# Filler products on TensorE: placed in waits up to 110 in the plan's time, or only up to 30

## The chip, the cores and the metric

One core of a Trainium2 chip runs the kernel. The metric is the device time of one execution in microseconds (us), read as the median of several runs of the same kernel.

## The reference

Attention over a pooled, projected key/value grid, and then a mixture of eight experts in which each token goes to one of them. Four batches of 12,288 tokens of 128 numbers; 768 keys per batch.

```python
kv_pool = kv.reshape(B, H // r, r, W // r, r, C).mean(axis=(2, 4))
k = v = kv_pool.reshape(B, -1, C) @ w_sr
s = scale * (q @ k.transpose(0, 2, 1))
a = np.exp(s - s.max(-1, keepdims=True)); a /= a.sum(-1, keepdims=True) + 1e-09
x = (a @ v).reshape(B * S, D)
logits = x @ w_gate; e = np.argmax(logits, axis=1); gate = softmax(logits)[e]
y = gate[:, None] * (np.maximum(x @ w1[e], 0.0) @ w2[e])
```

## The kernel before

The tokens are cut into 96 blocks of 512 (`block`, 24 per batch). For each block the scores against the 768 keys are made on TensorE in three steps of two products of 512 columns each (`scores`, written to a pair of PSUM banks `s`, of which there are two). ScalarE makes the exponential `e` of a pair (L1020), VectorE combines pair and exponential to `r` (L1022), and the values are then summed on TensorE into `po` (`values`). VectorE or ScalarE copy `po` out as `xp` (L1056, L1057), a transposing DMA turns it, and the expert's two layers follow on TensorE (`hidden`, `rows`, banks `b`, of which there are two as well). All matrix products but the transposes go through one helper, so they share line L387 and are told apart by their tiles.

Ahead of the blocks stands the preparation of batch 0: its keys are loaded, summed and turned (`keys`), giving `vT`, then `KT` (L548, VectorE), which the first scores need. The expert of the batch is guessed and its weights are loaded and rearranged (`expert`) while the first blocks already run: `b<-wg_raw,cbc` (the guess), `s<-ident,raw` (L694, the weights turned), `b<-kr` (a square of the keys), `b<-u,ones`, `b<-cg,vT`, `s<-Ms,raw`, and at about 80 us `PU` (L795, a 0/1 matrix that picks columns of the weights) with the products that gather through it.

The order of the work on every engine is fixed when the kernel is built. Each step is an `Op` with an engine, a planned duration and a due time; `Plan.order` runs a small simulation of the five engines and takes, engine by engine, the step that can start first. The times of this plan are its own, not the chip's.

Filler products belong to this plan. `fill` (L1526) makes three products of `slots16` with itself, 384 columns each, into a bank `b` that nobody reads. When `Plan.order` has picked the next step of TensorE with a start time `start` before `filler_end`, it first puts in as many groups of three as fit between the time at which TensorE becomes free and `start` (L208 to L221), at .487 us of plan time each. On the chip the fillers stand in TensorE's queue like any product: a real product behind them starts when they are through and when its own waits have ended. Each group takes one of the two banks `b` in the plan, so the choice of bank for later steps can swap.

```python
            if o.eng == "PE" and self.filler and start < self.filler_end:
                make, fill, us = self.filler
                while free["PE"] > self.filler_start:
                    i = min(range(len(slots["b"])), key=lambda i: slots["b"][i])
                    at = max(free["PE"], slots["b"][i])
                    if at + us > start:
                        break
```

Of the kernel before, what the change touches and what calls it, by code (L numbers as in the profile page):

```python
# [268 lines left out]
def attention_moe(ctx: ExitStack, tc, q, kv, w_sr, w_gate, w1, w2, out):  # L269
# [132 lines left out]
    plan = Plan({**SBUF, **PSUM})  # L402
# [3 lines left out]
    def buf(pool, shape, dtype=F32):  # L406
        where = psum if pool in PSUM else sb
        return Buf(pool, lambda name: where.tile(shape, dtype, name=name))

    def bank():  # L410
        return buf("b", [P, 512])
# [1115 lines left out]
        for _ in range(3):  # L1527
            mm(b.tile[:, :UN], slots16[:, :P], slots16, True, True)

    plan.filler, plan.filler_start, plan.filler_end = (bank().make, fill, .487), 9.0, 110.0  # L1530
    with tc.manual_schedule():
        plan.issue()

# [28 lines left out]
```

## Time and profile before

| what | value |
|---|---|
| time, median of 3 runs | 786.45 us (785.96 to 789.99) |
| the profiled execution's own time | 786.58 us |
| its span, first to last instruction | 784.5 us |
| granted TensorE clock, mean of the span | 0.998 |
| TensorE (PE) busy | 739.5 us, 94% |
| VectorE (DVE) busy | 639.1 us, 81% |
| ScalarE (ACT), GpSimd (POOL) busy | 588.0 us, 577.3 us |

The span is the profiled execution without launch and end, 2.1 us less than its time. Products are pipelined: a product's row gives the time from its start to its modelled end, so products that follow each other closely overlap in these rows, and the pace is read from their starts. The granted clock is a share of 2.4 GHz; 0.5 of it is the lower level, 1.2 GHz.

### The profile page before, as it was taken

The numbers are of one execution on the slowest core, as the hardware profiler recorded it, in microseconds if no ns is written. First come the engines' busy times: TensorE is split into PE (matmuls) and PEld (weight loads), VectorE is DVE, ScalarE is ACT, GpSimd is POOL, SyncE is SP. The second block draws the span as 40 slices with busy tenths as digits, with TensorE's granted clock in tenths as the row PEclk, the third lists the DMA queues.
The fourth block names the chain that finished last, engine by engine and source line by source line (L and its number), as shares of the span: only waits on it lengthen the run. The fifth ranks groups of instructions, "written<-read, shape, count | busy, mean of one in ns | idle before, by whom it ended". The sixth has DMA issues, their size and how long they took to land.

```text
span 784.5 us, 21744 instructions
## 1 busy us (share of the span) xinstructions
PE 739.5 (94%) x8399; PEld 580.3 (74%) x8399; DVE 639.1 (81%) x1262; ACT 588.0 (75%) x968; POOL 577.3 (74%) x803
## 2 busy tenths in 40 slices
PE   5997999999999899999999899999999999999995
PEld 5675776887777677778776776878877777787774
DVE  5789876889988888868968888688898898767685
ACT  1367778879778777777787787778878787878783
POOL 0357879878789888886779978888656957686662
PEclk9999999999999999999999999999999999999999
DMA  9676989995798999797569899799575889668441
GB/s 341 166 204 115 223 191 204 198 199 114 156 231 175 228 205 264 154 210 134 122 139 225 205 240 248 158 192 192 136 166 106 171 176 200 151 122 166 93 105 56
DMA packets 326168, 138.90 MB, mean 177 GB/s; under 512 B 212478, under 2 KB 318082, under 8 KB 326064
## 3 DMA queue, kind: packets, MB, share of 16 engines
q1 hardware_dynamic: 325584, 137.27, 78.0%
q8 instruction: 66, 1.08, 0.6%
q14 instruction: 38, 0.31, 0.1%
q0 software_dynamic: 192, 0.17, 0.1%
q10 hardware_dynamic: 288, 0.07, 0.0%
HBM read 59.12 MB, written 26.94 MB: 110 GB/s over the span
## 4 chain that ended last, share of the span: by engine, by line
PE 64%; DVE 9%; ACT 8%; DMA 8%; POOL 5%; issue 3%; SPq 0%; ACTq 0%; POOLq 0%; DVEq 0%
PE b L387 31%; PE po L387 19%; PE s L387 13%; DMA qT<-qp 4%; DVE r L1022 4%; ACT e L1020 3%; POOL kv L478 1%; DMA x<-xp 1%; DMA kv<-in_kv_dram 1%; DMA gp<-in_q_dram,gi 1%; ACT X L1113 1%; ACT g L1121 1%; DVE y L1148 1%; DVE xp L1057 1%; ACT junk L742 1%
## 5 line engine op out<-in xcount | busy, mean ns | idle before, releaser
L1022 DVE SCALAR_TENSOR_TENSOR r<-s,e 128x1024 bf16<-128x1024 f32 x288 | 346.8, 1217 | 63.7 <-ACT e L1020 61.6
L1020 ACT ACTIVATE e<-s 128x1024 f32<-128x1024 f32 x288 | 292.1, 1029 | 62.6 <-PE s L387 59.0
L387 PE MATMUL po<-v,r 128*128 128x145 f16 x2304 | 251.4, 227 | 2.6 <-DVE xp L1057 1.7
L387 PEld LDWEIGHTS <-r 128*128 128x128 bf16 x2304 | 167.0, 98 | 26.7 <-issue 4.9
L387 PE MATMUL s<-qT,KT 128*128 128x512 f16 x576 | 166.8, 379 | 11.6 <-DVE r L1022 7.7
L387 PE MATMUL b<-w2U,g 128*128 128x128 f16 x1664 | 156.5, 219 | 1.0 <-POOL g L1117 0.6
L387 PE MATMUL b<-x,w1U 128*128 128x512 f16 x465 | 139.4, 379 | 9.0 <-ACT g L1121 4.7
L387 PE MATMUL po<-M,qT 128*128 128x136 f16 x1152 | 130.9, 223 | 0.0
L387 PE MATMUL b<-L,x 128*128 128x128 f16 x1116 | 123.0, 219 | 1.1 <-ACT g L1121 0.7
L1003 POOL TENSOR_TENSOR qp<-qr,qp 128x512 f16<-128x512 f32 x94 | 108.9, 1159 | 15.6 <-DVE gi L1314 2.0
L1117 POOL TENSOR_TENSOR g<-X,g 128x512 f16<-128x512 f32 x94 | 108.8, 1158 | 10.8 <-DVE gg L1451 4.1
L387 PEld LDWEIGHTS <-g 128*128 128x128 f16 x1664 | 109.0, 98 | 1.9 <-POOL g L1117 1.4
L387 PEld LDWEIGHTS <-qT 128*128 128x128 f16 x1152 | 84.5, 98 | 27.6 <-issue 5.1
L1121 ACT ACTIVATE g<-b,zb 128x512 f16<-128x512 f32 x128 | 87.5, 692 | 18.3 <-PE b L387 15.3
L1001 POOL CAST qp<-qr 128x512 f16<-128x512 f32 x94 | 58.7, 625 | 47.7 <-DMA qr<-in_q_dram 25.3
L387 PEld LDWEIGHTS <-x 128*128 128x128 f16 x1116 | 80.9, 98 | 16.8 <-issue 5.4
L387 PEld LDWEIGHTS <-KT 128*128 128x128 bf16 x576 | 51.3, 99 | 48.0 <-issue 14.1
L1113 ACT ACTIVATE X<-b,zb 128x512 f32<-128x512 f32 x94 | 65.2, 696 | 19.5 <-PE b L387 19.5
L478 POOL TENSOR_TENSOR kv<-kv,kv 128x512 f32<-128x512 f32 x54 | 68.0, 1272 | 15.4 <-DMA kv<-in_kv_dram 6.1
L1115 POOL CAST g<-X 128x512 f16<-128x512 f32 x94 | 58.2, 620 | 28.3 <-ACT X L1113 13.1
L387 PEld LDWEIGHTS <-w1U 128*128 128x128 f16 x480 | 45.2, 98 | 40.5 <-issue 9.2
L1148 DVE TENSOR_TENSOR y<-b,gt 128x512 f32<-128x512 f32 x96 | 65.2, 680 | 7.8 <-PE b L387 5.8
(376 smaller groups left out, 961.2 us busy)
## 6 DMA issues: line engine op xcount, KB each, us to landing
qr<-in_q_dram SPq DMA_DIRECT2D x96, 256.0 KB, 3.4
out_dram<-y SPq DMA_DIRECT2D x96, 256.0 KB, 2.7
kv<-in_kv_dram SPq DMA_DIRECT2D x41, 512.0 KB, 6.1
raw<-in_moe_w_dram SPq DMA_DIRECT2D x14, 512.0 KB, 5.1
e<-in_kv_dram SPq DMA_DIRECT2D x3, 512.0 KB, 9.1
v_dram<-vT SPq DMA_DIRECT2D x4, 384.0 KB, 3.1
qT<-qp SPq DMA_TRANSPOSE x94, 3.6
x<-xp SPq DMA_TRANSPOSE x91, 3.5
```

Source lines behind the costliest of these rows:

```text
L387: return nc.tensor.matmul(o, l, r, start=start, stop=stop)
L478: nc.gpsimd.tensor_add(flat(to), flat(to), flat(of))
L742: op("ACT", 1.25, lambda j=j, junk=junk: nc.scalar.activation(junk.tile, krow.tile, AF.Sign, bias=key(j), scale=-1.0, accum_out=lc(j)), at ...
L1001: op("POOL", .62, lambda: nc.gpsimd.tensor_copy(qp.tile[:, 0], qr.tile), T - 1.9 * LEN, [("qr", t)], [("qh", t)], [qr, qp])
L1003: op("POOL", 1.17, lambda: nc.gpsimd.tensor_sub(qp.tile[:, 1], qr.tile, qp.tile[:, 0]), T - 1.8 * LEN, [("qh", t)], [("qp", t)], [qr, qp])
L1020: op("ACT", 1.03, lambda e=e, ps=ps: nc.scalar.activation(e.tile, ps.tile, AF.Exp), at + .6, [("s", t, s)], [("e", t, s)], [ps, e])
L1022: op("DVE", 1.22, lambda e=e, ps=ps, s=s: nc.vector.scalar_tensor_tensor(r.tile[:, 2 * s:2 * s + 2], ps.tile, 1.0, e.tile, op0=ALU.add, op ...
L1113: op("ACT", .69, lambda ph=ph, zu=zu: nc.scalar.activation(gf.tile, ph.tile, AF.Relu, bias=zu()), at + .5, [("ph", t, u), ("zb", b)], [("g ...
L1115: op("POOL", .62, lambda: nc.gpsimd.tensor_copy(gg.tile[:, 0], gf.tile), at + 1.5, [("gf", t)], [("gh", t), ("g", t)], [gf, gg])
L1117: op("POOL", 1.16, lambda: nc.gpsimd.tensor_sub(gg.tile[:, UH], gf.tile, gg.tile[:, 0]), at + 2, [("gf", t), ("gh", t)], [("g", t)], [gf, gg])
L1121: op("ACT", .69, lambda u=u, ph=ph, zu=zu: nc.scalar.activation(gg.tile[:, u], ph.tile, AF.Relu, bias=zu()), at + .5, [("ph", t, u), ("zb" ...
L1148: op("DVE", .69, lambda: nc.vector.tensor_tensor(y.tile, py.tile.rearrange("p (c d) -> p c d", d=C), bc(gr["gt"].tile[:, 0, js], C), op=AL ...
```

## The change

One number: `filler_end` goes from 110.0 to 30.0, in the plan's time. Steps of TensorE that start at 30 or later in the plan get no fillers ahead of them.

```diff
-    plan.filler, plan.filler_start, plan.filler_end = (bank().make, fill, .487), 9.0, 110.0
+    plan.filler, plan.filler_start, plan.filler_end = (bank().make, fill, .487), 9.0, 30.0
```

TensorE's queue has 28 groups of fillers before and 6 after: 22 groups, 66 products with their 66 weight loads, are left out. The other instructions of TensorE and all those of the other engines stand in the same order. From the place below on, the banks `b0` and `b1` are exchanged in all later steps, each for the other, with the same pattern of use.

TensorE's queue at the first scores of batch 0 (`u`: the scale of the keys; `KT`, `qT`: keys and queries of block 0; `slots`: the filler's operand), before:

```order
L387 LDWEIGHTS ones_b
L387 MATMUL b_325<-u_310,ones_b 128x128
L387 LDWEIGHTS slots_84
L387 MATMUL b_343<-slots_84 128x384
...
L387 MATMUL b_355<-slots_84 128x384
L387 LDWEIGHTS KT_338
L387 MATMUL s_359<-qT_295,KT_338 128x512
```

and with the change:

```order
L387 LDWEIGHTS ones_b
L387 MATMUL b_325<-u_310,ones_b 128x128
L387 LDWEIGHTS KT_338
L387 MATMUL s_343<-qT_295,KT_338 128x512
L387 LDWEIGHTS KT_338
```

Four groups (b_343, b_347, b_351, b_355) are gone, and the first scores stand right behind the product that they were separated from.

TensorE's queue between the guess of the expert and the third pair of scores (`qT_316`: queries of block 1), before:

```order
L387 MATMUL s_364<-qT_316,KT_338 128x512
L387 MATMUL b_372<-wg_raw,cbc_362 128x8
L387 LDWEIGHTS slots_84
L387 MATMUL b_402<-slots_84 128x384
...
L387 MATMUL b_414<-slots_84 128x384
L387 LDWEIGHTS KT_338
L387 MATMUL s_418<-qT_316,KT_338 128x512
```

and with the change:

```order
L387 MATMUL s_348<-qT_316,KT_338 128x512
L387 MATMUL b_356<-wg_raw,cbc_346 128x8
L387 LDWEIGHTS KT_338
L387 MATMUL s_386<-qT_316,KT_338 128x512
L387 LDWEIGHTS KT_338
```

Again four groups are gone. The same holds ahead of the next scores (1, 4, 1 and 3 groups), behind the values of block 0 (3 groups) and on both sides of a pair of scores just ahead of the gather through `PU` (1 and 1).

## Rows read from the trace of the kernel before

**Rows 1.** The page: the span, TensorE's share of it, and its granted clock.

```profile
span 784.5 us, 21744 instructions
...
PE 739.5 (94%) x8399; PEld 580.3 (74%) x8399; DVE 639.1 (81%) x1262; ACT 588.0 (75%) x968; POOL 577.3 (74%) x803
...
PEclk9999999999999999999999999999999999999999
```

**Rows 2.** Timeline of PE, 28 to 45 us: start, duration, line, tiles, count, [idle before].

```profile
28.51 0.23 PE L387 MATMUL b<-u,ones_b 128*128 128x128 bf16 x1 [0.20 <-DVE u L520]
29.22 2.33 PE L387 MATMUL b<-slots 128*128 128x384 f16 x12 [0.48 <-DVE con L523]
31.39 1.03 PE L387 MATMUL s<-qT,KT 128*128 128x512 f16 x4
32.25 0.28 PE L387 MATMUL b<-wg_raw,cbc 128*128 128x8 f32 x2
32.39 2.54 PE L387 MATMUL b<-slots 128*128 128x384 f16 x12
34.83 0.59 PE L387 MATMUL s<-qT,KT 128*128 128x512 f16 x2
...
36.39 2.11 PE L387 MATMUL b<-slots 128*128 128x384 f16 x12
38.34 0.59 PE L387 MATMUL s<-qT,KT 128*128 128x512 f16 x2
...
41.52 1.09 PE L694 MATMUL s<-ident,raw 128*128 128x128 f32 x8
```

**Rows 3.** Stretches: length, busy (instructions) of PE, PEld, DVE, ACT, POOL, clock, DMA, GB/s.

```profile
28.50:41.50 13.00, 12.25 (x66) 6.36 (x66) 11.68 (x28) 7.13 (x8) 8.21 (x11) 1.00 0.87 219
41.50:48.70 7.20, 6.91 (x63) 5.92 (x62) 4.93 (x12) 5.34 (x11) 2.79 (x4) 1.00 1.00 332
```

**Rows 4.** The same view for PE's filler products alone.

```profile
28.50:41.50 13.00, 9.73 (x51) 1.00 0.87 219
```

**Rows 5.** The chain of waits, 28 to 45 us: start, duration, what.

```profile
36.55 1.95 PE b L387 x12
```

**Rows 6.** Timeline of DVE: steps that TensorE waits for at 31.4, 38.3, 81.6 us.

```profile
30.04 1.07 DVE L548 TENSOR_SCALAR KT<-vT,con 128x256 bf16<-128x256 f32 x1
...
37.05 2.35 DVE L1022 SCALAR_TENSOR_TENSOR r<-s,e 128x1024 bf16<-128x1024 f32 x2
...
80.58 1.08 DVE L795 TENSOR_SCALAR PU<-slots,sg 128x384 f16<-128x384 f16 x4
```

**Rows 7.** Timeline of ACT and of DVE at 39 to 45 us.

```profile
39.20 1.92 ACT L1020 ACTIVATE e<-s 128x1024 f32<-128x1024 f32 x2
...
44.45 0.16 DVE L818 TENSOR_SCALAR ws<-b 128x2 f32<-128x2 f32 x1 [1.86 <-PE b L387]
```

**Rows 8.** Timeline of PE at 81 us.

```profile
81.14 0.65 PE L387 MATMUL b<-slots 128*128 128x384 f16 x3
81.62 0.61 PE L387 MATMUL b<-PU,w1l 128*128 128x128 f16 x8
```

**Rows 9.** Groups of PE, 8.4 to 13.05 us and 15.4 to 17.2 us: count, busy, mean ns, idle.

```profile
L387 PE MATMUL s<-ident,kv 128*128 128x128 f32 x20 | 4.9, 431 | 5.3 <-DVE kv L463 5.3
...
L387 PE MATMUL s<-ident,kv 128*128 128x128 f32 x16 | 1.9, 275 | 0.0
```

**Rows 10.** Timeline of PE, its last products.

```profile
778.39 0.61 PE L387 MATMUL b<-lp,ones 128*128 128x9 f32 x4
```

**Rows 11.** Stretches at the end of the span, columns as in rows 3.

```profile
775.00:780.00 5.00, 3.57 (x54) 3.13 (x51) 3.81 (x11) 0.00 (x0) 0.68 (x3) 1.00 0.16 44
780.00:785.00 5.00, 0.00 (x0) 0.00 (x0) 0.48 (x3) 0.00 (x0) 0.00 (x0) 0.61 0.21 66
```

**Rows 12.** PE's waits over the whole span: us in total, times, longest.

```profile
PE s L387 <- DVE r L1022: 7.7, 8, 1.7
...
PE s L387 <- DVE kv L463: 5.3, 1, 5.3
```

## The prediction

> **What bounds the kernel now.** I read the page first. TensorE (PE) is busy for 94% of the span and its clock row shows nines from end to end [rows 1]: over most of its length the kernel is paced by TensorE, and whatever delays it early is likely to be still there at the end. The change touches the first 82 us alone, so I went to the timeline of PE there, to see what stands around the fillers [rows 2]. Between 28.5 and 41.5 us TensorE is busy for 12.25 of 13 us [rows 3], but 9.73 us of that are 51 filler products [rows 4], 17 of the 22 groups that go. Real work is 15 products: the one at 28.51, four scores at 31.39, two at 32.25 and four pairs of scores, 0.23 + 1.03 + 0.28 + 4 x 0.59 = 3.9 us by their durations [rows 2]. So this stretch is not bound by TensorE.
>
> The chain of waits seems to say otherwise: it names a filler stretch, twelve products at 36.55, as part of the path [rows 5]. The reader should not believe it before looking at the other side of the wait. The scores at 38.34 [rows 2] reuse a bank pair that VectorE frees with the first of two steps that start at 37.05 and take 2.35 us together [rows 6]; half of that is 38.2, about 0.1 us ahead of the scores. VectorE releases them; the filler only happened to end last. From 41.5 to 48.7 us it is different: 6.91 of 7.2 us are real products [rows 3], without one filler, and VectorE sits idle for 1.86 us before it gets what it needs from there [rows 7]. That stretch is bound by TensorE.
>
> **The change, part by part.**
>
> *The products themselves.* In plan time 22 x .487 = 10.7 us of work go. They lay in waits, so I cost nearly all of it at nothing. The cover is the wait itself, and I look for places where the filler outlasts it. At 31.39 the first scores start [rows 2], while their keys are ready at 30.04 + 1.07 = 31.11 [rows 6]: at most 0.28 us, less the 0.1 us that a start takes behind its release at 38.34. At 81.62 the gather through PU starts behind a group that began at 81.14 [rows 8]; the gather's eight products need all pieces of PU, and the last four of these are done at 80.58 + 1.08 = 81.66 [rows 6]. Its eighth product starts at about 81.62 + 7 x 0.06 = 82.0 (the row's 0.61 us less a last product of some 0.2, over seven steps); without fillers it could start at about 81.75, so 0.25 us is the most that comes free. I take 0.2 us of gain in all; the ends are 0 (VectorE is just as late) and 0.5 (both places in full). The exchange of the two banks b0 and b1 changes no wait, for each keeps its partner's pattern: 0. The weight loads that go run beside the products: 0.
>
> *The clock.* This is the term that can cost. What the lower level is worth shows at the start of the span. The first 20 products of 128 columns, behind a wait of 5.3 us, take 431 ns each and fill 4.9 us, 0.24 us apiece; 16 of the same kind at 15.4 us take 275 ns and fill 1.9 us, 0.12 apiece [rows 9]. That is the pace of 1.2 GHz against 2.4 GHz, although the clock row shows full there as well (nothing is recorded ahead of the first change). It took from 8.4 to about 13 us of products before the pace rose.
>
> When does it fall? The trace shows one fall. The last products end at 778.39 + 0.61 = 779.0 [rows 10]; the granted clock is 1.00 up to 780 and 0.61 on average over the five us that follow [rows 11], which is 1.0 for 1.1 us and 0.5 for the rest. So it fell to 1.2 GHz at 781.1, 2.1 us after the last product. At the other end, no wait at full clock was longer than 1.7 us [rows 12], and none of those made it fall. The fillers gone, TensorE waits from 28.74 to about 31.3 us (2.6 us), from 32.5 to 34.83 (2.3 us), from about 36.5 to 38.34 (1.8 us) [rows 2], and again for shorter times. Two waits longer than the 2.1 us that sufficed at the end, one after another, with hardly any work between: I expect a fall somewhere between 31 and 36 us.
>
> A rule that speaks against this change stands in the Trainium skill, page "TensorE: Matmul & The Clock Gate", section "A second HAM failure mode: psum-queue depth-cycling": where products come in groups with short pauses between, the clock swings between its two levels although no pause is long. By that rule the sum holds the clock term below, and without it the gain of 0.2 us alone.
>
> *What the lower level costs.* First, the pairs of scores. Four columns' worth of 512 take 32.25 - 31.39 = 0.86 us [rows 2], 0.215 us each, so a pair ends 0.43 us later at half pace (an estimate by doubling). Most of this is hidden: the next exponential or VectorE's step has other work in front of it. Where it isn't is the pair at 38.34, whose exponential starts at 39.20 [rows 7]; the pair would end at 39.36 instead of 38.93 and the exponential start some 0.2 us late, and with it VectorE's step and the transposes at 41.52, which wait for that step's bank: +0.2 us (ends 0 and 0.4).
>
> Second, the stretch from 41.52, where TensorE has products without a gap and everybody waits for it. As long as the lower level lasts there, half of the time is lost. How long it lasts is the unknown. It could rise at once (0 lost), or need as long as at the start, 4.6 us, until 46.3 us: 2.3 us lost. I take 43.5 us, near the middle: 1.0 us lost. What is late then is the pair of scores at 42.65, the transposed weights' copy and VectorE's step at 44.45, and by them the values of block 0 at 48.8. Behind it both VectorE and TensorE are nearly full, so I let the 1.0 us through to the end.
>
> *The sum*: -0.2 + 0.2 + 1.0 = +1.0 us on the profiled execution's 786.58 us, 787.6 us. That execution is 0.13 us above the median of 786.45, so for the median I say **787.5 us**, 0.13% more. About 0.5% (3.9 us) is what a measurement of this kernel can tell from no change, so this would read as no difference.
>
> **The rivals.**
>
> *The clock stays up.* For it: all the new waits but two are shorter than the 2.1 us of idleness that stood ahead of the fall, and those two exceed it by little. Against it: no wait at full clock was longer than 1.7 us, so nothing shows that 2.6 us is borne. Then only the first term counts: 786.58 - 0.2 = 786.4 us, between 786.1 and 786.6.
>
> The same page of the Trainium skill, in "Why this matters for your kernels", warns of single idle gaps, and of long ones only. By that rule the clock would stay and this rival hold; the trace agrees in so far as 1.7 us did no harm.
>
> *Slower by more than 0.5%: the clock falls twice and comes back late.* The waits between 28.7 and 41.5 cost the whole of the unknown, 0.4 + 2.3 = 2.7 us with no gain. Then it falls again: three filler groups behind the values of block 0 go too, and a little later the scores wait for VectorE anyway (the 7.7 us in eight waits [rows 12]). A second return as slow as the first, 4.6 us with TensorE some two thirds busy, costs half of 3 us, 1.5 us. Together +4.2 us, 790.8 us. It decides from the point where the level is still low beyond 46 us and low again at a second place. Against it: behind 41.5 TensorE is as busy as it was at 8.4 to 13 us, so it should have recovered, and in the trace it kept its clock through all these later waits.
>
> *The change does something else than it says.* The order on all five engines speaks against it: only fillers are gone. What is left is chance in the transfers when everything shifts by a fraction of a us, which I can't price; within 1 us either way.
>
> **How the numbers follow.** The clock falls once, 786.8 to 789.1 us (the sum with both ends of its unknowns): 0.58. It stays up, 786.1 to 786.6: 0.32. It falls twice or for long, 789.1 to 791: 0.08. Something else: 0.02. The range from 785.9 to 789.3 takes in the first two cases with a little for the scatter of the runs (the lowest of three was 785.96) and leaves out the third. Slower by over 0.5%, past 790.4, is most of the third case: 0.06. Faster by over 0.5% would need 3.9 us from fillers that free 0.5 at most: 0.01. Within 0.5%: 0.93.
>
> **What would show it.** Right: the profile after shows TensorE idle for 2 us and more at 29 and 33 us; a stretch with a granted clock of 0.5 that begins between 31 and 36 and ends between 41 and 47 us; products at 41.5 of 128 columns with 400 ns and more instead of 270; the values of block 0 about 1 us later than 48.8, and the distance kept to the end. Wrong: the clock at 1.00 throughout (the first rival; values of block 0 at 48.8 or earlier), a second stretch at 0.5 behind 50 us (the second), or a delay at 48.8 us that is gone by the end, which would mean that VectorE and not TensorE paces what follows.

## The result, and the profile after

The change takes 793.52 us (median of 6 runs, 790.4 to 796.92); the kernel before, run beside it, 787.31 us (785.96 to 789.99). The ratio is 1.007, 95% interval 1.0045 to 1.0096: slower by 0.7%, 6 us. The forecast of 787.5 us, no change, was wrong, and so was its range, 785.9 to 789.3. The profiled execution is one of the slower ones, 796.42 us, so the 9.8 us between the two profiles' spans are more than the change itself.

The page of the change; in [rows 1] the same three lines:

```profile
span 794.3 us, 21610 instructions
...
PE 738.1 (93%) x8333; PEld 580.5 (73%) x8333; DVE 638.7 (80%) x1262; ACT 588.6 (74%) x968; POOL 577.0 (73%) x803
...
PEclk9779999999999999999999998999999999999999
```

TensorE does less, 738.1 us against 739.5, and the span is longer. The clock row has sevens in the second and third slice and an eight in the 25th. The view of stretches gives the places (the clock is the column behind POOL):

```profile
28.50:41.50 13.00, 6.55 (x16) 1.98 (x15) 10.73 (x28) 6.42 (x8) 7.43 (x11) 0.58 0.78 219
41.50:48.70 7.20, 6.22 (x39) 5.32 (x40) 3.04 (x8) 6.03 (x11) 0.97 (x2) 0.57 1.01 310
30.70:47.70 17.00, 11.43 (x45) 6.30 (x46) 10.83 (x22) 11.50 (x16) 6.86 (x10) 0.50 0.82 235
68.20:71.70 3.50, 3.27 (x24) 2.68 (x25) 3.47 (x7) 2.35 (x4) 2.81 (x4) 0.51 0.33 75
481.20:488.10 6.90, 6.44 (x29) 4.18 (x29) 4.20 (x10) 4.26 (x6) 5.86 (x10) 0.51 0.88 188
```

The first two answer to [rows 3]: TensorE's clock there is 0.58 and 0.57 in place of 1.00. The lower level lies at 30.7 to 47.7 us, again at 68.2 to 71.7, and late in the span at 481.2 to 488.1. The timeline of PE shows what stood ahead of each fall; [rows 2] are its counterpart:

```profile
28.82 0.23 PE L387 MATMUL b<-u,ones_b 128*128 128x128 bf16 x1 [0.20 <-DVE u L520]
31.19 1.89 PE L387 MATMUL s<-qT,KT 128*128 128x512 f16 x4 [2.14 <-DVE KT L548]
32.87 0.43 PE L387 MATMUL b<-wg_raw,cbc 128*128 128x8 f32 x2
35.61 2.17 PE L387 MATMUL s<-qT,KT 128*128 128x512 f16 x4 [2.30 <-DVE r L1022]
39.10 2.14 PE L387 MATMUL s<-qT,KT 128*128 128x512 f16 x4 [1.33 <-DVE r L1022]
42.48 1.97 PE L694 MATMUL s<-ident,raw 128*128 128x128 f32 x8 [1.24 <-DVE r L1022]
...
51.91 0.24 PE L387 MATMUL po<-v,r 128*128 128x145 f16 x1
...
66.38 0.59 PE L387 MATMUL s<-qT,KT 128*128 128x512 f16 x2 [1.14 <-DVE r L1022]
68.43 1.03 PE L387 MATMUL s<-qT,KT 128*128 128x512 f16 x2 [1.45 <-DVE r L1022]
...
480.49 0.61 PE L387 MATMUL s<-qT,KT 128*128 128x512 f16 x2 [1.82 <-DMA qT<-qp]
```

and in the kernel before, the same view at three of these places:

```profile
48.77 0.24 PE L387 MATMUL po<-v,r 128*128 128x145 f16 x1
...
63.47 0.59 PE L387 MATMUL s<-qT,KT 128*128 128x512 f16 x2 [1.14 <-DVE r L1022]
65.51 0.61 PE L387 MATMUL s<-qT,KT 128*128 128x512 f16 x2 [1.45 <-DVE r L1022]
```

The first scores end the wait of 2.14 us at 31.19, 0.20 us sooner than before, and find the clock low: four columns' worth of 512 take 32.87 - 31.19 = 1.68 us, 0.86 in [rows 2]. The transposes of the weights stand at 42.48 (41.52 before), the values of block 0 at 51.91 (48.77). The waits ahead of the products at 66.38 and 68.43 are the kernel's own, to the hundredth; of these two traces only the change's shows a fall of the clock there (whether the change makes it is asked below, from the traces of other kernels). The wait for `qT`, the transposed queries, at 480.49 has no counterpart: 472.88 in the trace of before, without a wait.

How late TensorE is after all that: start of a product in a trace minus start of the same product in the first trace of before, in us, at times of that trace (all kernels are told of below).

| at | change | change again | e3 | e6 | e8 | before again | e10 | e11 | e14 |
|---|---|---|---|---|---|---|---|---|---|
| 30 | -0.2 | -1.3 | -0.6 | 1.2 | -0.4 | -0.5 | 0.4 | -0.5 | -0.4 |
| 50 | 3.1 | 1.1 | 2.5 | 3.3 | -0.4 | -0.5 | 0.4 | 0.1 | 2.7 |
| 110 | 4.3 | 2.1 | 3.4 | 3.1 | -0.4 | -0.5 | 0.5 | 2.1 | 2.5 |
| 290 | 5.8 | 4.2 | 3.4 | 3.3 | 0.2 | 0.1 | -0.3 | 0.1 | 0.6 |
| 530 | 8.1 | 5.0 | 1.9 | 3.4 | 3.4 | -1.4 | 2.2 | -1.0 | 0.2 |
| 770 | 9.8 | 7.4 | 3.8 | 3.9 | 4.2 | -0.1 | 2.7 | -0.4 | 0.8 |

In the change 4.3 us are lost by 110 us (the last group that the edit takes out stood at 81 us), and another 5.5 behind it, where the two programs are the same. The early loss has an evident suspect, the clock. The late one has none in the prediction: it comes in steps, at waits for transposing transfers. The view of PE's waits over the span, of before (one more line of [rows 12]: us in total, times, longest) and then of the change:

```profile
PE s L387 <- DMA qT<-qp: 3.2, 4, 1.1
```

```profile
PE s L387 <- DVE r L1022: 11.7, 12, 2.3
PE s L387 <- DMA qT<-qp: 7.3, 6, 1.8
...
PE s L387 <- DVE KT L548: 2.1, 1, 2.1
```

### The profile page after: what moved, and what is told of

Same layout as the page of the kernel before. It is cut to its first block, busy times and chain, and to the rows that moved or that the text cites. A ratio compares the mean times of both kernels' runs of the same rounds, so it can differ in the third digit from the quotient of the medians.

```text
span 794.3 us, 21610 instructions
## 1 busy us (share of the span) xinstructions
PE 738.1 (93%) x8333; PEld 580.5 (73%) x8333; DVE 638.7 (80%) x1262; ACT 588.6 (74%) x968; POOL 577.0 (73%) x803
## 4 chain that ended last, share of the span: by engine, by line
PE 67%; DVE 10%; ACT 9%; DMA 7%; issue 3%; POOL 2%; SPq 0%; ACTq 0%; DVEq 0%; POOLq 0%
PE b L387 31%; PE po L387 20%; PE s L387 14%; DVE r L1022 4%; DMA qT<-qp 4%; ACT e L1020 4%; DMA x<-xp 2%; ACT g L1121 2%; DMA e<-in_kv_dram 1%; ACT X L1113 1%; DVE y L1148 1%; DVE xp L1057 1%; ACT xp L1056 1%; ACT g L1125 1%; POOL kv L478 1%
## 5 line engine op out<-in xcount | busy, mean ns | idle before, releaser
L1022 DVE SCALAR_TENSOR_TENSOR r<-s,e 128x1024 bf16<-128x1024 f32 x288 | 347.3, 1218 | 71.7 <-ACT e L1020 68.9
L387 PE MATMUL s<-qT,KT 128*128 128x512 f16 x576 | 171.1, 388 | 21.5 <-DVE r L1022 11.6
```

The costliest lines, as they stand in the source:

```text
L387: return nc.tensor.matmul(o, l, r, start=start, stop=stop)
L1022: op("DVE", 1.22, lambda e=e, ps=ps, s=s: nc.vector.scalar_tensor_tensor(r.tile[:, 2 * s:2 * s + 2], ps.tile, 1.0, e.tile, op0=ALU.add, op ...
```

## The experiments

Each time stands against runs of the kernel before in the same series on the same chip. Single runs of one kernel lay up to 9 us apart, so verdicts rest on medians and intervals.

### Which of the removed groups matter: e1, e2, e4

In e1 the last 5 of the 22 groups go, in e4 all but the first 4, which stand in the first wait:

```diff
-    plan.filler, plan.filler_start, plan.filler_end = (bank().make, fill, .487), 9.0, 110.0
+    plan.filler, plan.filler_start, plan.filler_end = (bank().make, fill, .487), 9.0, 45.0
```

(This is against the kernel before; e4 has 32.0 in place of 45.0.) In e2 the 17 early groups go and the last 5 stay:

```diff
-            if o.eng == "PE" and self.filler and start < self.filler_end:
+            if o.eng == "PE" and self.filler and start < self.filler_end and not 30.0 <= start < 45.0:
```

> Leaves out only the last five of the 22 filler groups (three behind the values of block 0, two at 80 us); the 17 in the waits from 29 to 41.5 us stay. Theory C (the lower clock from 30.7 to 47.7 us costs the time): no fall before 50 us, values of block 0 within 0.2 us of 48.8, a fall at 65 to 72 us possible; 786 to 789 us, ratio 0.998 to 1.003. Rival P (each group left out costs its share, by the pace of the order and not by the clock): 5/22 of 6.2 us, 788.7 us, with the clock at 1.00.

> The other part of the change alone: the 17 groups in the waits from 29 to 41.5 us go, the last five stay. Theory C: the clock falls at 30 to 36 us and returns at 41 to 48, values of block 0 at 51 to 52 us, 790 to 793 us, ratio 1.004 to 1.008; most of the change's loss. Rival P: 17/22 of 6.2 us, 792 us, but with the loss where the clock is full. Rival F (the loss comes from the falls behind 60 us, which the last five groups prevent): 788 us.

> Only the four groups in the first long wait (29.2 to 31.4 us) stay of the 22. Theory C: the clock is full at 31 us and falls at 33 to 38 us, since the waits behind are as thin; it returns at 44 to 48; values of block 0 at 50 to 51.5 us, 788.5 to 792 us. Rival W (only the first wait, the longest, makes it fall): clock 1.00 up to 60 us, values of block 0 at 48.8, 786 to 788 us.

| kernel | median us (runs) | before | ratio (95%) | clock low, us |
|---|---|---|---|---|
| e1 | 790.78 (12) | 788.45 | 1.0023 (1.0005 to 1.0042) | only at 776 |
| e2 | 798.09 (6) | 788.45 | 1.0110 (1.0083 to 1.0137) | 29.0 to 46.1 |
| e4 | 794.68 (9) | 788.45 | 1.0073 (1.0048 to 1.0099) | 35.9 to 46.2, 66.7 to 70.1 |

The early clock loss belongs to the 17 early groups. With them the clock stays up (e1); without them it falls in the first wait (e2, the first trace of the change), and with the first four alone it falls behind the next one, 2.30 us for `r` (e4, at 35.9 us). But e1, whose clock never falls ahead of 776 us, is slower too, and its trace is not late until about 470 us, and lastingly only from 650 us on. Something is lost that has nothing to do with the clock.

Two of the expectations missed in size. e2 has 1.0110 where 1.004 to 1.008 was expected: it lost 9.6 us, more than the change itself, though it takes out fewer groups. e4, at 794.68 us, lies above the 788.5 to 792 that were expected. The clock alone does not give such sums.

### The same waits, nearly empty products in them: e3

The 22 groups stay, with 8 columns a product:

```diff
-                    w.eng, w.us, w.fn, w.at, w.gives, w.needs, w.lands = "PE", us, (lambda b=b: fill(b)), 0.0, ["fill"], (), 0.0
+                    w.eng, w.us, w.fn, w.at, w.gives, w.needs, w.lands = "PE", us, (lambda b=b, n=UN if start < 30.0 else 8: fill(b, n)), 0.0, ["fill"], (), 0.0
...
-            mm(b.tile[:, :UN], slots16[:, :P], slots16, True, True)
+            mm(b.tile[:, :n], slots16[:, :P], slots16[:, :n], True, True)
```

> All 22 groups stay in TensorE's queue, with their weight loads, banks and waits, but each product has 8 columns where it had 384. Theory C, if the products' own length is what holds the clock: falls as with the change, 791 to 796 us, ratio 1.005 to 1.010. Rival P (the queue, the banks or the places of the instructions matter): as before, 786 to 788 us. If the clock holds although the products are short, 786 to 788 us with 1.00 at 30 to 48 us: then the weight loads are enough.

Measured: 790.59 us (12 runs) against 788.45, 1.0019 (0.9998 to 1.0039). The stretches of its trace:

```profile
29.50:46.50 17.00, 12.35 (x85) 7.91 (x83) 11.47 (x23) 11.06 (x13) 7.63 (x10) 0.50 0.83 231
67.00:70.40 3.40, 2.62 (x18) 2.03 (x19) 3.37 (x7) 2.90 (x4) 2.64 (x3) 0.50 0.30 70
```

The clock falls as in the change, for as long, twice. Its trace is 3.1 us later at 50 us than at 30, and 3.4 late at 110: the early loss is all there. Behind that hardly anything is added. So the empty waits' clock costs some 2 us in the median (the interval just takes in no loss at all; 1.005 to 1.010 was expected), and the change loses three times as much. What e3 has in common with before, and not with the change, is the number of instructions on TensorE (66 products and 66 weight loads fewer in the change) and the banks b0 and b1 of all later steps.

### Banks, count or chance: e6, e7, e8 and before again

Three theories for the late part: **banks** (their exchange), **shift** (TensorE's program is shorter, so that its instruction loads, a DMA queue of their own in the trace, fall at other places of the work), **chance** (it differs from run to run).

e6 is e3, but its groups take no bank in the plan:

```diff
+                held = list(slots["b"]), free["PE"]
...
+                if start >= 30.0:
+                    slots["b"], free["PE"] = held
```

e7 is before with b0 and b1 exchanged from the start:

```diff
+        slots["b"][0] = 0.01
```

e8 is before, with 6 products of 192 columns in each of the 22 groups (n is 6 there, 3 in the others):

```diff
-    def fill(b):
-        for _ in range(3):
-            mm(b.tile[:, :UN], slots16[:, :P], slots16, True, True)
+    def fill(b, n):
+        for _ in range(n):
+            mm(b.tile[:, :UN * 3 // n], slots16[:, :P], slots16[:, :UN * 3 // n], True, True)
```

> As e3 (the 66 removed products stay at their places with 8 columns, so that TensorE's program is as long as before), but the groups take no bank in the plan, so that every later step has the bank (b0 or b1) that it has in the change. Left to settle is the late part of the loss, the 2 to 6 us that build up after 110 us in the change, e1 and e4 and hardly in e3. Theory shift (the late loss comes because TensorE's program is 132 instructions shorter, so that its instruction loads fall at other places of the work): as e3, 1 to 3.5 us over the run before of the same chip, with an early fall of the clock and a lateness that grows by less than 1.5 us after 110 us. Rival banks (it comes from the swapped banks): as the change, 5 to 7.5 us over, with late steps of 3 to 6 us. Rival chance: the late part differs from run to run and not from kernel to kernel, so that this gives anything from 2 to 6.

> The kernel before with all 28 groups at their full size, and b0 and b1 exchanged from the start; nothing else. Theory shift: within 1 us of before, no fall of the clock before 400 us. Rival banks: 2 to 5 us over, all of it after 110 us. Rival chance: within 1 us in the median over all runs.

> The kernel before, but its 22 groups from 30 on in the plan have six products of 192 columns in place of three of 384: the same columns, so that the clock should stay up, the same banks, and 132 instructions more in TensorE's program, as many as the change has less. Theory shift: no fall of the clock before 400 us, and a late loss as in e1, 1.5 to 4 us, at waits for transposing transfers after 110 us. Rivals banks and chance: within 1 us of before.

> The kernel before itself, unchanged, as a measure of chance. All theories: within 0.5 us of the runs before of the same chip in the median (its single runs lay 7 us apart). Its profile shows what of the late waits comes by chance: theory shift and theory banks want its lateness against the first profile of before within 1.5 us all the way; rival chance wants steps of 2 us or more at waits for transposing transfers.

| kernel | median us (12 runs) | before | ratio (95%) |
|---|---|---|---|
| e6, banks of the change, count of before | 791.02 | 788.42 | 1.0026 (1.0005 to 1.0047) |
| e7, banks of the change, clock and count of before | 788.33 | 788.42 | 1.0001 (0.9980 to 1.0022) |
| e8, 132 instructions more, full fillers | 790.41 | 788.42 | 1.0022 (1.0001 to 1.0044) |
| e9, before again | 788.93 | 788.42 | 1.0012 (0.9988 to 1.0036) |

Banks falls, within the 0.2% that the intervals leave: e7 equals before, and e6, with the change's banks and clock but before's count, equals e3. Chance is there: before against itself moved by 0.5 us in the median and 1.6 us along the trace, and e6 and the second trace of the change had a fall of the clock at 450 and 451.7 us that no other trace has. But it does not place the waits. The loss of e8 is small, its interval hardly clear of none, but its trace is plain. It has the full clock through all the early stretch (first line), and still the waits of the change:

```profile
28.50:48.50 20.00, 19.18 (x181) 15.88 (x181) 16.25 (x40) 12.49 (x18) 11.00 (x14) 1.00 0.94 265
476.40:479.70 3.30, 3.30 (x20) 2.69 (x18) 2.79 (x6) 1.70 (x3) 3.13 (x5) 0.50 0.77 172
```

```profile
251.85 0.61 PE L387 MATMUL s<-qT,KT 128*128 128x512 f16 x2 [1.16 <-DMA qT<-qp]
...
474.70 0.60 PE L387 MATMUL s<-qT,KT 128*128 128x512 f16 x2 [1.86 <-DMA qT<-qp]
```

The change has the same waits, 1.18 us at 257.48 and 1.82 at 480.49, and the clock is low for a while behind the longer one in both. The wait ahead of the same two products in every kernel that ran, those of the sections below among them (us, from each trace; 111.85 and 250 to 252 are the times in before):

| kernel | instructions against before | at 111.85 | at 250 to 252 |
|---|---|---|---|
| before, again; e7; e3; e6 | 0 | 1.10, 1.25; 1.00; 1.25; 1.25 | 0, 0; 0.44; 0.43; 0.27 |
| e10 | +256 | 0.68 | 0 |
| the change, again | -132 | 0, 0 | 1.18, 1.80 |
| e8 | +132 | 0 | 1.16 |
| e4; e2 | -108; -102 | 0; 0 | 1.18; 1.21 |
| e1 | -30 | 0 | 0.42 |
| e11, e14 | +64 | 0, 0 | 0, 0 |
| e12 | +192 | 0 | 0 |

The wait at 111.85 is there in every kernel with before's count, whatever its clock and its banks, and in none with another, but for e10. The wait at 472.88 is nearly the reverse: 0.4 to 1.9 us in the change (both traces), e1, e2, e4, e8 and e14, under 0.15 in all other traces.

Behind the wait at 472.88 is a transfer that an instruction load has met. The view of DMAs over the life of one transfer, the `qT` issued at 469.5 us in before (then the change, at 475.7; then e8, at 469.9):

```profile
q1 hardware_dynamic: 3106, 1.01, 110.6%
issues: line engine op xcount, KB each, median us to landing
qr<-in_q_dram SPq DMA_DIRECT2D x1, 256.0 KB, 3.3
x<-xp SPq DMA_TRANSPOSE x2, 5.1
qT<-qp SPq DMA_TRANSPOSE x1, 3.4
```

```profile
q1 hardware_dynamic: 3089, 1.00, 122.7%
q8 instruction: 1, 0.02, 1.2%
...
qT<-qp SPq DMA_TRANSPOSE x1, 4.7
```

```profile
q1 hardware_dynamic: 3044, 0.98, 118.6%
q8 instruction: 1, 0.02, 1.2%
...
qT<-qp SPq DMA_TRANSPOSE x1, 4.7
```

In the change and in e8 there is one packet of queue q8, 0.02 MB of instructions, 1.8 us behind the issue, and the same transfer takes 4.7 us in place of 3.4. The page counts 66 or 67 such packets in every one of these kernels. Taken together over the 14 traces other than e14's: 173 transposing transfers had such a load between 0.5 us ahead of their issue and 3 us behind it in some of the traces and not in others; with it they landed 0.70 us later on average (worked out from issues, landings and packets).

### Is it the place of the loads? e10, e11, e12 and the change again

In the time of before, the loads of the change and of e8 (132 instructions fewer and 132 more) stand at the same places as each other, half a spacing from those of before (whose own are 7 to 16 us apart behind 46 us, 12 in the median). So about 264 instructions make a spacing, and the place can be set by cutting the same filler columns into more products, as in e8 with n from a list. e10 (256 instructions more), e11 (64) and e12 (192):

```diff
+    plan.parts = iter([9] * 18 + [8] * 4)
...
+    plan.parts = iter([5] * 10 + [4] * 12)
...
+    plan.parts = iter([8] * 8 + [7] * 14)
```

> The kernel before with the same filler columns cut into more products: the 22 groups from 30 on in the plan have 9 or 8 products (128 or 144 columns) in place of three, 128 products in all and so 256 instructions more on TensorE. The trace of before has 66 instruction loads of 16 KB on their own DMA queue, 10 to 15 us apart; those of the change and of e8 (132 fewer and 132 more) stand at the same places of the work as each other (117.8, 250, 472, 649 us in the time of before) and half a spacing from those of before, e9, e7, e3 and e6 (108.7, 243 and 255, 479, 643 and 656). So 264 instructions are about one spacing, and 256 move the loads by one whole spacing. Theory shift by place of the loads: they stand as in before again, the wait for qT at 111.8 us of before (1.10 us) is there, those at 251 and 473 (1.2 and 1.8 us in the change and e8) are not; 0 to 1 us over before, no fall of the clock before 400 us. Rival length (any change in the count or in the products costs something): waits at 251 and 473 as in e8, 1.5 to 4 us over. Rival chance: waits at places that none of the earlier profiles has.

> As e10, but with 32 products and so 64 instructions more: the loads a quarter of a spacing earlier than in before (about 106, 252.5, 476, 653 us). Theory shift: the late lateness is neither that of before nor that of e8; the wait at 111.8 us goes if the load must come within 5 us ahead of the transfer, and the time lies between 1.5 us under and 3 us over before. Rival length: 0.5 to 3 over. Rival chance: as before within 1 us. Should it be faster than before by 1 us or more, it is a version that beats both kernels.

> As e10, but with 96 products and so 192 instructions more: the loads three quarters of a spacing earlier than in before (about 112, 246 and 258, 470 and 482, 647 us). Theory shift: again a lateness of its own, between 1.5 us under and 3 us over before; a wait for x at 649 us as in e1, e2 and e4, whose loads stand at 648.4 to 649. Rival length: 1.5 to 4 over. Rival chance: as before within 1 us.

> The change itself once more, on the chip of the other runs, for a second profile of it and a time beside theirs. Theory shift: 5 to 7.5 us over before; the lower clock from about 30 to 47 us and again near 68; waits for qT near 251 and 473 us of before's time as in its first profile, and no wait at 111.8; 2 to 5 us more than e3 and e6. Rival chance: late waits at other places than in the first profile, and a time within 1.5 us of e3 and e6.

| kernel | median us (runs) | before | ratio (95%) | PE's waits for `qT` in its trace |
|---|---|---|---|---|
| e10, a whole spacing | 788.58 (12) | 788.78 | 0.9997 (0.9976 to 1.0018) | 2.3 us in 5 |
| e11, a quarter | 785.55 (12) | 788.78 | 0.9954 (0.9935 to 0.9973) | 1.2 us in 3 |
| e12, three quarters | 790.61 (12) | 788.78 | 1.0021 (0.9996 to 1.0046) | 2.8 us in 4, and 1.3 for `x` |
| e13, the change | 794.57 (6) | 788.78 | 1.0078 (1.0047 to 1.0109) | 5.2 us in 6, and 2.1 for `x` |

e10 decides against rival length, which e12 by itself would have fitted: the most products of all, and the time of before, with before's wait at 111.94 us (0.68) and none for `qT` at 251 and 473. Its one big step, 2.9 us at 491, is a wait for a gather (3.09 us, 1.71 in before), near whose end the clock fell, which no theory here foretold. e11 is the version that **beats both kernels**, 0.5% under before and 1.1% under the change, more than the 1.5 us that were expected at best, though in its profile the clock fell at 66.6 to 70.0 us with all fillers in place. That profiled execution, 787.19 us, was among its slowest, so the column of e11 above shows little of the gain. e12's wait for `x` came where it was expected, 1.31 us at 650.72, but before again has one of 0.76 us ahead of the same product. The change repeated its time; its waits stood at the same places, 1.80 us at 255.82 and 0.72 at 479.42. So the places are the program's, the size differs between runs.

### Do the two parts add up? e14

e14 is e11 with 8 columns a product in the 22 groups:

```diff
+            m = UN if n == 3 else 8
+            mm(b.tile[:, :m], slots16[:, :P], slots16[:, :m], True, True)
```

> As e11 (the 22 groups have 98 products in place of 66, TensorE's program is 64 instructions longer than before), but those products have 8 columns, so that the clock falls as in the change. If the two losses add up, the one by the clock (e3 and e6: 1.9 and 2.6 us over before) and the one by the place of the instruction loads (e11: 3.2 under), this lies 0 to 1.5 us under before, 0.995 to 1.001 of it, some 6 us under the change, with the lower clock from about 30 to 47 us, no waits for qT at 251 and 473 us of before's time, and no wait at 111.8. Rival: the late loss comes of the early lateness (work that is late by 3 us meets transfers otherwise), and the place of the loads matters only beside it; then the late waits come back here and it lies 2 to 6 us over before.

Measured: 788.4 us (12 runs) against 788.48, 0.9999 (0.9983 to 1.0015). Clock and waits:

```profile
29.60:46.70 17.10, 13.19 (x115) 8.82 (x114) 11.53 (x24) 11.06 (x13) 7.73 (x10) 0.50 0.87 223
```

```profile
PE s L387 <- DVE r L1022: 10.7, 12, 1.7
PE s L387 <- DMA qT<-qp: 1.1, 3, 0.5
```

The clock falls as in the change, the wait at 111.85 is gone, 0.45 us is left at 474, and the late waits do not come back. So they don't need the early lateness. In this run the two parts add up: with the change's clock and e11's place of the loads the kernel is where it was before. Against e11, with the same count and the clock full at 30 to 47 us, e14 is slower by 2.9 us from median to median (ratios 0.9999 and 0.9954): a third size for the early loss beside the 2.1 of e3 and the 2.6 of e6.

## Why the prediction was wrong

**What bounds the kernel** was read right: a delay that enters ahead of 50 us was still there at the end in e3, e6 and the change, and e14 ends later than e11; VectorE did not take it up.

**The products themselves: right.** The first scores stood 0.28 us behind the end of VectorE's step for their keys (31.39, 31.11), and stand 0.06 behind it with the change (31.19, 31.13): 0.22 us came free. At the gather nothing did: TensorE is 4.3 us late at 75 us and at 90. That the start by the span is sooner by 0.20 us too is luck, for the product ahead of it (28.82, 28.51) came 0.31 later.

**When the clock falls: right in the place, 30.7 us against "between 31 and 36" (31.8 in the change again), and not for the reason given.** The first rival, that the clock stays up, is out. But the length of a wait, 2.1 us as at the end of the span, is not what decides. The change's clock fell 1.6 us into its wait of 2.14, and 1.7 us is what the kernel before bears. In the change again the wait of 2.27 us passed at full clock, and the level fell 0.6 us into the next, of 2.33. In e3 it fell at 29.5 with no wait over 0.5 us just ahead, among the fillers of 8 columns. The traces show thin work around each of these falls, and not how thin it has to be.

By the section "Why this matters for your kernels" of "TensorE: Matmul & The Clock Gate" in the Trainium skill, which warns of long single gaps, the clock would have stayed; the measurement decides against it here. By the rule of the same page of the Trainium skill that spoke against the change ("A second HAM failure mode: psum-queue depth-cycling": short pauses between groups of products) the clock can fall without a long wait; the fall in e3 and the one at 68.2 us, behind 1.14 and 1.45 us, agree with it, though the same two waits passed at full clock in 9 of the 15 traces.

**The step that failed first: how long the lower level lasts.** The prediction said "I take 43.5 us, near the middle: 1.0 us lost", by the 4.6 us of products that it had seen ahead of the rise at the start. The level stayed until 47.7, beyond its upper end of 46.3. From the first transposes, 42.48, that is 5.3 us (4.2 to 5.3 in the seven traces with this fall): the 4.6 us were about right, and taking the middle between them and nothing had no row behind it. And its cost began before 41.52: the term of +0.2 us for the pairs of scores measured 42.48 - 41.52 = 0.96, for the pairs from 31 us on ran at half pace, and VectorE did less in the same stretch, 10.73 us against 11.68 [rows 3]. The rest is 51.91 - 48.77 = 3.14 less 0.96, 2.2 us. In place of +1.0, the three terms make +3.1 by 51.91. In the change again the level was back at 45.5, inside the range, and still 2.4 us were lost between 30 and 50 us.

**The rival "falls twice", given 0.08, came true in part by luck.** Its sign, a level still low beyond 46 us and low again at a second place, is in the first trace of the change (47.7 and 68.2). The second fall cost 1.2 us by the table (3.1 to 4.3), where the rival had 1.5. But that fall is not shown to come of the change: e11 and e12 have it with all filler columns in place, and e2, e6 and e14, whose clock was low in the early stretch as well, do not. This whole early part is worth about 2 to 3 us in the medians (e3, e6, e14 against e11), which would still have read as no difference.

**The step that failed most was the smallest: "chance in the transfers when everything shifts by a fraction of a us ... within 1 us either way".** It was no chance and no fraction of a us: 132 instructions fewer moved TensorE's instruction loads half a spacing against the work behind 82 us, and other transposing transfers met them. By itself (e8, whose loads stand where the change's do) that costs 2.0 us, ratio 1.0022 (1.0001 to 1.0044). "The order on all five engines speaks against it: only fillers are gone", so that the rest costs nothing, was the assumption that failed: the order is the same, but not the place of the loads in it.

The sum of the parts, 0.19 to 0.26% and 0.22%, is less than the change's 0.70 to 0.78%. The intervals are about 0.2% wide to either side, and e14 against the change (0.9999 against 1.0078) puts the place of the loads at more than e8 does. No run takes 132 instructions out at full clock, so the remaining 2 us are not assigned by a run. The traces say where they are likely to lie. All of TensorE's waits for DMAs together (the lines `qT`, `x` and `gp` of the waits view) are 4.2 to 5.6 us in the five traces with before's count and in e10, 7.8 and 8.8 in the change, 8.1 in e8, 7.1 in e4, 9.9 in e2, and 2.3 and 1.8 in e11 and e14. The change's surplus over the five, 3.7 us on average, and the 2 to 3 us of the clock make its 6. These are single executions, and two kernels don't fit: e1 (4.0) and e12 (4.6) are slower by 2.3 and 1.8 us without such a surplus, and why stays open. Not tried: moving the transposing transfers in the plan away from the loads.

## What to carry to other kernels

Fillers in TensorE's waits paid for themselves through the clock here, by 2 to 3 of 788 us, because real products without a gap follow. Look at the stretch behind the waits, and price the lower level until the trace shows it gone, with all the work in front of it. When instructions are added or taken out of a long program, look where its instruction loads stand against the transfers of the work: here all the rest moved against them. Before a difference under 1% is credited to an edit, run it once with the count made up again (nearly empty products here), and try two or three counts, for that alone was worth from -0.5% to +0.2%.

## What was not expected of the hardware

- A load of 16 KB of instructions beside a transposing transfer lengthened it: 3.4 us without one, 4.7 with one at the same place in two kernels, and 0.70 us on average over 173 transfers. The clock fell behind the longest of the waits that came of it in the change (0.51 in 481.2 to 488.1 us) and in e8, but not behind 1.80 us at 255.82 in the change again, nor behind 1.82 us at 422.42 in e12.
- Once down near 30 us the clock stayed at 0.50 for 17 us in the change, e2, e3 and e14, but for 10 to 14 in e4, e6 and the change again; in the falls at 65 to 72 us it stayed for 3.4.
- The wait of 1.45 us for VectorE at 65 to 68 us stands in all 15 traces; the clock fell there in the change (both traces), e3, e4, e11 and e12, and not in the others, e14 and e2 among them, which had been low ahead of it too. The wait of 1.72 us for VectorE at 446 us of before's time stands in all 15 as well; the clock fell just behind it in e6 and the change again alone. What else decides was not found.
